# Attention scores as float32 matmuls of 64 rows in place of split operands of 128 rows

## The chip, the core and the metric

The kernel runs on one core of one Trainium2 chip. The metric is the device time of one execution in microseconds (us); the text gives the median of several runs. TensorE (PE in the rows; PEld is its weight load) multiplies matrices, VectorE (DVE), ScalarE (ACT) and GpSimd (POOL) work element by element, and the queue of SyncE (SP) issues nearly all transfers.

## The reference

Attention with a learned position bias feeds two gated feed-forward layers. Only the first part is touched by the change:

```python
B, H, S, D = q.shape                      # 2, 8, 576, 64
scores = np.matmul(q, k.transpose(0, 1, 3, 2)) / np.sqrt(D)
x = (log1p(abs(i - j)) / log1p(max(i, 1)))[..., None]
bias = np.maximum(x @ w1 + b1, 0.0) @ w2   # 32 hidden columns, one result for each head
scores = scores + bias.transpose(2, 0, 1)[None]
attn = softmax(scores)                     # over the last axis
out = np.matmul(attn, v)                   # then two gated layers, 512 -> 1536 -> 512
```

## The kernel before

Two heads form a pair, so a batch has four pairs (`hp` 0 to 3). The 576 rows of queries are cut into blocks, `it` 0 to 3 of 128 rows and `it` 4 of the last 64. A unit of work is a batch, a pair and a block: 40 units, the 20 of batch 0 first, with block 4 ahead of the others (`ITS`, L33; `UNITS`, L239 to L242). In a unit of 128 rows each of the two heads is a job `j`; in a unit of block 4 the two heads lie side by side in one tile of 128 rows.

The operands come from the array `qk`, which holds the 64 rows of a head's transposed queries (or keys) twice, one copy in partitions 0 to 63 and one in 64 to 127. `load_raw` (L122) issues one transfer for the queries and one for the keys of a pair. `split_set` (L140) then makes three float32r tiles: `qs`, whose upper half of partitions is the rounded query and whose lower half is the remainder, `kh`, the rounded key in both halves, and `kl`, the key's remainder in both halves. That is a copy each for `qs` and `kh` (L136 on ScalarE, L138 on GpSimd) and three subtractions (L150) for each pair and batch; `SPLIT0`, `SPLIT1` and `BOT0` say in which turn they are queued and on which engine, and `drain(poolq, ...)` issues them a few at a time. The raw tiles have one buffer of their own, and two more are borrowed from the tag `pt`.

`qk_mm` (L267) makes the scores. For 128 rows it issues four float32r matmuls for each job (L288): contraction 128, 128 columns of stationary `qs`, 288 moving columns of `kh`, then of `kl`, for each half of the keys. For block 4 it issues four plain float32 matmuls of contraction 64 from the raw tile (L276), the two heads going to the two halves of the output's partitions, that is, of the array's columns. A float32 matmul stands in the trace as two MATMUL records, a float32r one as one. The scores of one job take two of the four banks of the pool `ps2`.

A loop over turns `n` (L660) issues the parts of several units in an order written out by hand (`ORDERS`, L49): `M` adds scores and bias and takes the minimum on VectorE (L301), `X` is the exponential on ScalarE (L322), `N` the normalisation (L330, L332, and on GpSimd L334), `T` transposes unit n-3 on TensorE (L360), `E` takes the transposes out of PSUM, `P` and `V` are the product with the values (L380), `Q0` and `Q1` are the scores of unit n+1, `S0` and `S1` issue split work, `B` loads the bias of unit n+2, `L` loads operands, and `A`, `b`, `c` are steps of the position bias.

The bias is made once, for batch 0 and 1 together, in 36 groups of 16 rows: four hidden tiles a group, mostly on VectorE (L194), four matmuls (L208), a way out of PSUM (L212), a mirrored copy, mostly on GpSimd (L223), and a write to DRAM (L226), from which units read their rows (`bt`). Seven steps go ahead of the loop (`PRE`), the rest into turns 0 to 12. From turn 21 on, `C` converts the float64 weights of the layers to split float32 (L449 to L472). After the last unit come the 72 steps of the layers (L487, L512).

Every engine works its instructions off in the order in which they are issued.

Of the kernel before, what the change touches and what calls it, by code (L numbers as in the profile page):

```python
# [31 lines left out]
# order of the blocks of rows: the last 64 rows come first  # L32
ITS = (4, 0, 1, 2, 3)  # L33
# engines of the position bias: step -> hidden columns on ScalarE and on GpSimd (else VectorE);
# groups whose result leaves PSUM, or is mirrored, on VectorE (else ScalarE, GpSimd)
# [5 lines left out]
# turns of the attention loop that load and split operands: by pair of heads  # L41
RAW0 = {1: -3, 2: -2, 3: 1}
SPLIT0 = {0: -2, 1: -3, 2: -1, 3: 1}
BOT0 = ("gpsimd", "vector", "vector", "gpsimd")
LOAD1 = {10: 0, 20: 1, 24: 2, 29: 3}
SPLIT1 = {16: 0, 20: 1, 25: 2, 30: 3}
LOADV = {2: (0, 0), 3: (0, 1), 4: (0, 2), 5: (0, 3), 22: (1, 0), 25: (1, 1), 28: (1, 2), 32: (1, 3)}
# order in which a turn of the attention loop issues its parts
ORDERS = [  # L49
# [4 lines left out]
]  # L54
# float64's high word of the smallest normal float32, read as a float32
# [3 lines left out]
def rows_of(it):  # L59
    return 128 if it < 4 else 64  # L60


def bias_width(it):
    # distances j - i of a block of rows
    return S + rows_of(it) - 1
# [3 lines left out]
def fused_kernel(ctx: ExitStack, tc: tile.TileContext, qk, vp, tab, pcol, invp, prm, wts, rg, out):  # L69
# [18 lines left out]
    first = ExitStack()  # L88
    sb = first.enter_context(tc.tile_pool(name="sb", bufs=2, side="right"))
# [17 lines left out]
    # the tensor engine's clock rises with use: keep it busy until the first operands land  # L107
# [9 lines left out]
    # scores = [q_hi; q_lo] . [k_hi; k_hi] + [q_hi; q_lo] . [k_lo; k_lo]  # L117
    sets = {}
    raws = {}
    poolq = []  # L120

    def load_raw(b, hp, which, tag="raw", eng=nc.sync):  # L122
        if which == 0:
            raws[b, hp] = (wk if tag == "raw" else w2).tile([128, 4, S], F32, tag=tag, name=f"raw{b}{hp}", bufs=1 if tag == "raw" else 2)
        eng.dma_start(raws[b, hp][:, 2 * which : 2 * which + 2], qk[b, hp, which])
# [8 lines left out]
    def copy(o, i, eng):  # L134
        if eng == "act":
            nc.scalar.activation(o, i, AF.Copy)  # L136
        else:
            nc.gpsimd.tensor_scalar(o, i, 1.0, 1.0, op0=ALU.mult, op1=ALU.mult)  # L138

    def split_set(b, hp, copies, kl_eng, bot_eng):  # L140
        raw = raws[b, hp]
        qr, kr = raw[:, 0:2], raw[:, 2:4]
        pool = sb if b == 0 and hp >= 2 else wk
        qs = pool.tile([128, 2, S], F32R, tag="qs", name=f"qs{b}{hp}")
        kh = pool.tile([128, 2, S], F32R, tag="kh", name=f"kh{b}{hp}")
        kl = pool.tile([128, 2, S], F32R, tag="kl", name=f"kl{b}{hp}")
        sets[b, hp] = (qs, kh, kl)

        def low(o, i, h, eng):
            getattr(nc, eng).tensor_tensor(o, i, h.bitcast(F32), op=ALU.subtract)  # L150

        items = (
            lambda: copy(qs, qr, copies[0]),
            lambda: copy(kh, kr, copies[1]),
            lambda: low(qs[64:128], qr[64:128], qs[64:128], bot_eng),
            lambda: low(kl[:, 0], kr[:, 0], kh[:, 0], kl_eng[0]),
            lambda: low(kl[:, 1], kr[:, 1], kh[:, 1], kl_eng[1]),
        )
        poolq.extend(items)

# [5 lines left out]
    load_raw(0, 0, 0)  # L166
    load_raw(0, 0, 1)
# [5 lines left out]
    hts = {}  # L173

    # distances j - i from c0 on that a group's rows need on the longer side of the diagonal;
    # the bias depends on the distance's size only, so the other side is a mirror image
# [70 lines left out]
    def load_bias(n):  # L247
        b, hp, it = UNITS[n]
        bt = wk.tile([128, 2, S], F32, tag="bt", name=f"bt{n}", bufs=3)
        # row i starts i places to the left of the row before it  # L250
        w = bias_width(it)
        r = rows_of(it)
        flat = bias_d[it].rearrange("a w -> (a w)")
        for h in range(2 if it == 4 else 1):
            o = r - 1 + (2 * hp + h) * w
            rows = flat[o : o + r * (H * w - 1)].rearrange("(i k) -> i k", k=H * w - 1)
            if it == 4:
                nc.sync.dma_start(bt[h * 64 : h * 64 + 64, 0], rows[:, :S])
            else:
                nc.sync.dma_start(bt, rows[:, : 2 * w].rearrange("i (a k) -> i a k", a=2)[:, :, :S])  # L260
        st[n, "bt"] = bt

    # the last 64 rows of a pair's two heads go side by side: one tile of 128 rows
    def jobs(n):
        return 1 if UNITS[n][2] == 4 else 2

    def qk_mm(n, j):  # L267
        if j >= jobs(n):
            return
        b, hp, it = UNITS[n]  # L270
        sp = bank2(f"s{n}_{j}")
        if it == 4:
            raw = raws[b, hp]
            for hf in range(2):
                for h in range(2):
                    nc.tensor.matmul(  # L276
                        sp[h * 64 : h * 64 + 64, hf, :288],
                        raw[:64, h, 512:],
                        raw[:64, 2 + h, hf * 288 : hf * 288 + 288],
                        start=True,  # L280
                        stop=True,
                    )
        else:
            qs, kh, kl = sets[b, hp]
            lhs = qs[:, j, it * 128 : it * 128 + 128]
            for i, kk in enumerate((kh, kl)):
                for hf in range(2):
                    nc.tensor.matmul(  # L288
                        sp[:, hf, :288], lhs, kk[:, j, hf * 288 : hf * 288 + 288], start=(i == 0), stop=(i == 1)
                    )  # L290
        st[n, "s", j] = sp
# [151 lines left out]
    # float64 bits to float32: exponent and mantissa shifted into place, the low word's  # L443
    # rounded top bits added, values below the normal range set to zero
# [55 lines left out]
    def out_mm(s):  # L500
# [27 lines left out]
        # a bank's matmuls come before its readers, but at the end the readers run ahead  # L528
# [82 lines left out]
    # pieces go through a load and four steps, the steps of one turn each on another piece;  # L611
    # `limit`: pieces that have a free slot
# [18 lines left out]
    def raw0(n):  # L631
        for hp in range(1, 4):
            if RAW0[hp] == n:
                for i in range(2):
                    load_raw(0, hp, i, "raw" if hp == 3 else "pt")

    def split0(n):
        for hp in range(4):
            if SPLIT0[hp] == n:
                split_set(0, hp, ("act", "act" if hp == 0 else "pool"), ("gpsimd", "gpsimd"), BOT0[hp])  # L640

    raw0(-3)
    for i in range(PRE):
        bias_step()
        if i == 3:
            nc.vector.tensor_scalar(w1l[:, S:], w1l[:, S:], prms[:, 0:1], None, op0=ALU.mult)
            split0(-3)
        if i == 4:
            load_bias(0)
            qk_mm(0, 0)  # L650
            raw0(-2)
            split0(-2)
        if i == 6:
            load_bias(1)
            raw0(-1)
            split0(-1)
        if i > 3:
            drain(poolq, 3)

    for n in range(NU + TL + 1):  # L660
# [13 lines left out]
        def load_new():  # L674
            if n in LOAD1:
                for i in range(2):
                    load_raw(1, LOAD1[n], i)
            if n in LOADV:
                load_v(*LOADV[n])
            raw0(n)  # L680
            split0(n)
            if n in SPLIT1:
                split_set(1, SPLIT1[n], ("act", "pool"), ("vector", "gpsimd"), "gpsimd")

        def steps(k):
# [4 lines left out]
        dq = 3 if n < 25 else 2  # L690
# [17 lines left out]
            "Q0": lambda: n + 1 < NU and qk_mm(n + 1, 0),  # L708
            "Q1": lambda: n + 1 < NU and qk_mm(n + 1, 1),
            "S0": lambda: drain(poolq, dq - dq // 2),  # L710
            "S1": lambda: drain(poolq, dq // 2),
# [9 lines left out]
        if n == NB0:  # L721
            first.close()
            open_ring("mc", range(EARLY), "right")
# [110 lines left out]
```

## Time and profile before

| | |
|---|---|
| median of 3 runs | 691.87 us (688.51 to 692.51) |
| span of the profiled execution | 689.6 us |
| busy TensorE | 655.5 us, 95% |
| busy VectorE | 510.2 us, 74% |
| busy GpSimd | 354.4 us, 51% |
| busy ScalarE | 329.7 us, 48% |
| transfers | 87.06 MB, mean 126 GB/s |

For the profiled execution only its span is listed; the median of the runs is 2.3 us above it. A matmul's record includes its way through the array, and records overlap, so busy TensorE is not TensorE at its limit. Shares of the whole span are means over stages: the position bias and batch 0 (up to about 133 us), batch 1 (to about 209 us) and the layers (to the end).

### The profile page before, as it was taken

Reading aid. Unit: us, or ns where it says so; the run is one execution under the profiler, and the core shown is the slowest. Engines: PE = TensorE matmul, PEld = TensorE weight load, DVE = VectorE, ACT = ScalarE, POOL = GpSimd, SP = SyncE. Lnnn points to the kernel's source line nnn. Section 1 sums busy time; section 2 is a strip of 40 time slices with the busy share of each in tenths; the row PEclk is TensorE's granted clock in tenths of the full one; section 3 lists DMA queues with packets and bytes.
Section 4 is the critical chain, followed back from the end, with each engine's and each line's share of the span. In section 5 each row is a group of like instructions: output and inputs, shape, how many; then the busy total and the mean of one; then the engine's idle time right before and its main releaser. Section 6 shows DMA issues by size and latency. Waiting matters only on the chain.

```text
span 689.6 us, 11697 instructions
## 1 busy us (share of the span) xinstructions
PE 655.5 (95%) x4290; PEld 584.3 (85%) x4290; DVE 510.2 (74%) x941; ACT 329.7 (48%) x685; POOL 354.4 (51%) x336
## 2 busy tenths in 40 slices
PE   8779999988799799999999999989999999999997
PEld 4215567876678799989999999989999999999997
DVE  7899997578898986997677687989988778420121
ACT  5536678978786443444333345475443433211111
POOL 4557655889967453444434356665644444211111
PEclk9799999999999999999999999999999999999999
DMA  6659877689752332243223222232222221000111
GB/s 231 208 168 308 283 253 259 207 287 322 226 188 87 128 121 94 93 124 121 69 85 121 94 62 66 87 88 67 92 88 68 90 93 31 1 1 1 47 46 47
DMA packets 31641, 87.06 MB, mean 126 GB/s; under 512 B 3552, under 2 KB 5216, under 8 KB 31584
## 3 DMA queue, kind: packets, MB, share of 16 engines
q1 hardware_dynamic: 30720, 85.14, 37.9%
q10 hardware_dynamic: 864, 1.18, 0.5%
q8 instruction: 34, 0.56, 0.3%
q14 instruction: 23, 0.19, 0.1%
HBM read 73.05 MB, written 13.25 MB: 125 GB/s over the span
## 4 chain that ended last, share of the span: by engine, by line
PE 66%; DVE 17%; issue 5%; DMA 5%; ACT 3%; POOL 3%; SPq 0%; POOLq 0%; DVEq 0%; ACTq 0%
PE gv L487 35%; PE pv L380 4%; DVE ht L194 3%; PE tp L360 3%; PE s L288 3%; PE bps L208 3%; DVE ab L467 2%; DVE t L301 1%; DVE ff L460 1%; DMA bt<-bias_d 1%; DMA bias_d<-be 1%; DVE wv L472 1%; DVE tt L449 1%; DVE wl L472 1%; DVE rb L462 1%
## 5 line engine op out<-in xcount | busy, mean ns | idle before, releaser
L497 POOL TENSOR_TENSOR gl<-g,gh 128x384 fp32r<-128x384 f32 x72 | 89.2, 1239 | 180.7 <-ACT gh L495 180.7
L493 DVE TENSOR_TENSOR g<-gv,sg 128x384 f32<-128x384 f32 x72 | 40.0, 556 | 133.7 <-PE gv L487 122.6
L463 POOL TENSOR_TENSOR ff<-ff,rb 128x512 int32<-128x512 int32 x72 | 95.1, 1321 | 80.7 <-DVE rb L462 76.5
L495 ACT ACTIVATE gh<-g 128x384 fp32r<-128x384 f32 x72 | 37.9, 526 | 127.3 <-DVE g L493 126.6
L487 PE MATMUL gv<-xh,wl 128*128 128x384 f32 x240 | 80.8, 337 | 1.2 <-DVE wl L472 1.2
L487 PE MATMUL gv<-xh,wh 128*128 128x384 f32 x240 | 81.2, 338 | 0.0
L487 PE MATMUL gv<-xl,wh 128*128 128x384 f32 x240 | 80.7, 336 | 0.0
L334 POOL TENSOR_SCALAR p<-p,rs 128x576 f32<-128x576 f32 x72 | 65.1, 916 | 16.7 <-DVE rs L332 12.4
L194 DVE TENSOR_SCALAR ht<-w1l,bpc 128x448 f32<-128x448 f32 (+17 forms) x131 | 73.1, 624 | 0.3
L467 DVE SCALAR_TENSOR_TENSOR ab<-ab,ff 128x512 f32<-128x512 f32 x72 | 69.1, 959 | 0.0
L491 ACT ACTIVATE sg<-gv 128x384 f32<-128x384 f32 x72 | 35.0, 486 | 70.0 <-PE gv L487 69.5
L487 PE MATMUL gv<-nh,wh 128*128 128x384 f32 x192 | 64.8, 337 | 0.0
L468 ACT ACTIVATE wh<-ab 128x512 fp32r<-128x512 f32 x54 | 34.2, 633 | 63.9 <-DVE ab L467 63.6
L208 PE MATMUL bps<-ht,prms 128*32 128x264 f32 (+17 forms) x352 | 54.7, 530 | 10.5 <-DVE ht L194 8.6
L487 PE MATMUL gv<-nl,wh 128*128 128x384 f32 x192 | 64.5, 336 | 0.0
L487 PE MATMUL gv<-nh,wl 128*128 128x384 f32 x192 | 64.5, 336 | 0.0
L322 ACT ACTIVATE p<-t,mn 128x576 f32<-128x576 f32 x72 | 55.4, 770 | 13.1 <-DVE mn L301 11.2
L472 DVE TENSOR_TENSOR wl<-ab,wh 128x512 fp32r<-128x512 f32 x54 | 58.2, 1079 | 0.0
L462 DVE TENSOR_SCALAR rb<-wr 128x512 int32<-128x512 uint32 x72 | 56.9, 791 | 0.0
L301 DVE CUSTOM_DVE_ANT_0 t<-s,bt 128x576 f32<-128x576 f32 x72 | 51.7, 750 | 6.0 <-DMA bt<-bias_d 3.0
L460 DVE SCALAR_TENSOR_TENSOR ff<-wr,tt 128x512 uint32<-128x512 uint32 x72 | 54.3, 754 | 0.0
L360 PEld LDWEIGHTS tp<-ident,p 128*128 128x128 f32 (+1 forms) x328 | 36.0, 142 | 18.7 <-issue 6.7
(418 smaller groups left out, 1642.3 us busy)
## 6 DMA issues: line engine op xcount, KB each, us to landing
wr<-wts SPq DMA_DIRECT2D x72, 512.0 KB, 3.6
bt<-bias_d SPq DMA_DIRECT2D x32, 576.0 KB, 5.0
bias_d<-be SPq DMA_DIRECT2D x36, 295.5 KB, 3.2
raw<-qk SPq DMA_DIRECT2D x16, 576.0 KB, 5.6
v<-vp SPq DMA_DIRECT2D x8, 480.0 KB, 6.0
bt<-bias_d SPq DMA_DIRECT2D x16, 144.0 KB, 4.0
out<-part SPq DMA_DIRECT2D x6, 192.0 KB, 1.9
out<-part ACTq DMA_DIRECT2D x6, 192.0 KB, 1.9
```

The source lines that it names most:

```text
L194: nc.vector.tensor_scalar(ht, src, bpc[:, t : t + 1], 0.0, op0=ALU.add, op1=ALU.max)
L208: nc.tensor.matmul(ps[cg * 32 : cg * 32 + 32, :cut], prms[:, 2:34], hs[cg][:, a : a + cut], start=True, stop=True)
L301: nc.vector.tensor_tensor_reduce(t, sp[:, :, :288], bt[:, j].rearrange("p (a c) -> p a c", a=2), -SCALE, 3.0e38, ALU.add, ALU.min, mn[:, j ...
L334: nc.gpsimd.tensor_scalar(p[:, j], p[:, j], rs[:, j : j + 1], 1.0, op0=ALU.mult, op1=ALU.mult)
L360: nc.tensor.transpose(tp[:k, x * 128 : x * 128 + 128], blocks[i + x], ident)
L460: nc.vector.scalar_tensor_tensor(ff, hw, 0xC0000000, tt, op0=ALU.bitwise_and, op1=ALU.bitwise_or)
L462: nc.vector.tensor_scalar(rb, lw, 2.0**-29, None, op0=ALU.mult)
L463: nc.gpsimd.tensor_tensor(ff.bitcast(I32), ff.bitcast(I32), rb, op=ALU.add)
L467: nc.vector.scalar_tensor_tensor(ab, ab, TINY_HI, ff.bitcast(F32), op0=ALU.is_ge, op1=ALU.mult)
L472: nc.vector.tensor_tensor(lo, ab, hi.bitcast(F32), op=ALU.subtract)
L487: nc.tensor.matmul(ps[:, :CH], wt[:, cs], xt[:, cc, :], start=(k == 0), stop=(k == 11))
L497: nc.gpsimd.tensor_tensor(gl, g32, gh.bitcast(F32), op=ALU.subtract)
```

## The change

The split is gone, with its queue, its tiles, the pool `sb` and the parts `S0` and `S1`. `load_raw` now puts the queries and keys of a pair's first head into partitions 0 to 63 and those of its second head into 64 to 127 of one tile, half as many bytes, still in two transfers a pair; there are six such buffers. The loads of pair 3 of batch 0 move from turn 1 to ahead of the loop, those of pair 1 of batch 1 from turn 20 to turn 18. All scores are plain float32 matmuls of contraction 64: the first head on rows 0 to 63 of the array, the second on rows 64 to 127. `Q0` and `Q1` become one part `Q` that stands where `Q0` stood, except that `M1` now follows `M0` in three of the four orders.

```diff
-RAW0 = {1: -3, 2: -2, 3: 1}
-SPLIT0 = {0: -2, 1: -3, 2: -1, 3: 1}
-BOT0 = ("gpsimd", "vector", "vector", "gpsimd")
-LOAD1 = {10: 0, 20: 1, 24: 2, 29: 3}
-SPLIT1 = {16: 0, 20: 1, 25: 2, 30: 3}
+RAW0 = {1: -3, 2: -2, 3: -1}
+LOAD1 = {10: 0, 18: 1, 24: 2, 29: 3}
...
-    "M0 T X0 M1 N E0 B E2 E1 A L Q0 S0 X1 Q1 S1 P0 P1 b c V C",
-    "C M0 T L M1 X0 E0 Q0 X1 E2 A E1 B Q1 N P0 S0 P1 b V c S1",
-    "M0 X0 M1 C T Q0 N E1 E2 A B L E0 X1 Q1 P0 b S0 S1 P1 V c",
-    "M0 T X0 E2 N A Q0 E0 M1 C Q1 X1 E1 B L P0 S0 b P1 V S1 c",
+    "M0 M1 T X0 N Q E0 B E2 E1 A L X1 P0 P1 b c V C",
+    "C M0 M1 T L X0 E0 Q X1 E2 A E1 B N P0 P1 b V c",
+    "M0 M1 X0 C T Q N E1 E2 A B L E0 X1 P0 b P1 V c",
+    "M0 T X0 E2 N A Q E0 M1 C X1 E1 B L P0 b P1 V c",
...
+    def load_raw(b, hp):
+        t = wk.tile([128, 2, S], F32, tag="raw", name=f"raw{b}{hp}", bufs=6)
+        raws[b, hp] = t
+        for h in range(2):
+            r = slice(h * 64, h * 64 + 64)
+            nc.sync.dma_start(t[r], qk[b, hp][:, r, h].rearrange("w p s -> p w s"))
...
+    def qk_mm(n):
         b, hp, it = UNITS[n]
-        sp = bank2(f"s{n}_{j}")
+        raw = raws[b, hp]
+        sps = [bank2(f"s{n}_{j}") for j in range(jobs(n))]
         if it == 4:
...
+            order = [(h, hf, sps[0][h * 64 : h * 64 + 64, hf, :288]) for h in range(2) for hf in range(2)]
         else:
...
+            order = [(h, hf, sps[h][:, hf, :288]) for hf in range(2) for h in range(2)]
+        for h, hf, dst in order:
+            r = slice(h * 64, h * 64 + 64)
+            nc.tensor.matmul(
+                dst,
+                raw[r, 0, it * 128 : it * 128 + rows_of(it)],
+                raw[r, 1, hf * 288 : hf * 288 + 288],
+                start=True,
+                stop=True,
+            )
```

## Rows read from the trace of the kernel before

**Rows 1.** Windows by stage: us, busy time (instructions) by engine, TensorE's clock, DMA share, GB/s.
```profile
12.10:63.80 51.70, 41.91 (x250) 15.00 (x245) 48.77 (x91) 25.48 (x48) 33.39 (x30) 0.87 0.64 206
103.00:133.00 30.00, 29.66 (x295) 23.45 (x293) 20.42 (x65) 25.82 (x64) 19.85 (x26) 1.00 0.67 219
133.00:209.00 76.00, 67.94 (x628) 53.59 (x626) 63.17 (x160) 61.42 (x158) 64.30 (x72) 1.00 0.76 254
140.00:200.00 60.00, 51.94 (x465) 39.79 (x465) 52.80 (x131) 46.28 (x118) 51.20 (x53) 1.00 0.83 271
209.00:689.60 480.60, 468.63 (x2689) 462.13 (x2686) 333.25 (x510) 182.61 (x338) 208.62 (x163) 1.00 0.24 76
```

**Rows 2.** Timeline of VectorE, 12 to 64 us: start, duration, what, count.
```profile
12.74 3.43 DVE L194 TENSOR_SCALAR ht<-w1l,bpc 128x576 f32<-128x576 f32 x3
18.88 3.71 DVE L194 TENSOR_SCALAR ht<-w1l,bpc 128x560 f32<-128x560 f32 x3
22.59 1.32 DVE L194 TENSOR_SCALAR ht<-w1l,bpc 128x544 f32<-128x544 f32 x3
...
35.53 4.38 DVE L194 TENSOR_SCALAR ht<-w1l,bpc 128x480 f32<-128x480 f32 x4
...
45.36 8.18 DVE L194 TENSOR_SCALAR ht<-w1l,bpc 128x432 f32<-128x432 f32 x12
```

**Rows 3.** Timeline of GpSimd over the same stretch.
```profile
14.35 3.08 POOL L150 TENSOR_TENSOR kl<-raw,kh 128x576 fp32r<-128x576 f32 x2
19.11 2.76 POOL L150 TENSOR_TENSOR qs<-raw,qs 64x1152 fp32r<-64x1152 f32 x1 [1.68 <-ACT qs L136]
...
36.56 3.08 POOL L150 TENSOR_TENSOR kl<-raw,kh 128x576 fp32r<-128x576 f32 x2
...
48.82 2.62 POOL L150 TENSOR_TENSOR qs<-raw,qs 64x1152 fp32r<-64x1152 f32 x1
```

**Rows 4.** The splits by source line: duration min/median/max in ns, first and last start.
```profile
L150 POOL TENSOR_TENSOR kl<-raw,kh x12: 1399/1464/1849, 14.3 to 185.5; 128x576 fp32r<-128x576 f32 x12
L150 POOL TENSOR_TENSOR qs<-raw,qs x6: 2622/2634/3054, 19.1 to 180.1; 64x1152 fp32r<-64x1152 f32 x6
L150 DVE TENSOR_TENSOR kl<-raw,kh x4: 740/752/1294, 125.8 to 177.9; 128x576 fp32r<-128x576 f32 x4
L150 DVE TENSOR_TENSOR qs<-raw,qs x2: 1355/1356/1356, 17.5 to 40.1; 64x1152 fp32r<-64x1152 f32 x2
L138 POOL TENSOR_SCALAR kh<-raw x7: 1142/1157/1587, 12.9 to 175.9; 128x1152 fp32r<-128x1152 f32 x7
L136 ACT ACTIVATE qs<-raw x8: 1152/1157/1164, 14.2 to 175.6; 128x1152 fp32r<-128x1152 f32 x8
```

**Rows 5.** The chain that ended last, 40 to 64 us: start, us, what.
```profile
40.90 6.61 DMA raw<-qk
...
59.59 1.50 POOL kl L150
...
62.79 5.12 DMA bias_d<-be
```

**Rows 6.** Timeline of TensorE, one full turn near 121 us; block 4 at 144 us.
```profile
120.55 1.20 PE L360 MATMUL tp<-ident,p 128*128 128x128 f32 x9
121.51 0.51 PE L288 MATMUL s<-kh,qs 128*128 128x288 f32 x2
...
122.75 1.31 PE L380 MATMUL pv<-pt,v 128*64 128x128 f32 x20
123.99 1.20 PE L360 MATMUL tp<-ident,p 128*128 128x128 f32 x9
...
144.54 1.19 PE L276 MATMUL s<-raw 64*64 64x288 f32 x8 [1.01 <-DVE mn L301]
145.66 1.31 PE L380 MATMUL pv<-pt,v 128*64 128x128 f32 x20
```

**Rows 7.** Transfers by line: size of one, median us from issue to landing.
```profile
raw<-qk SPq DMA_DIRECT2D x16, 576.0 KB, 5.6
```

More of the change, by code (lines that the diff above doesn't have):

```diff
@@ L87, in fused_kernel @@
     wk = attn.enter_context(tc.tile_pool(name="wk", bufs=2))
-    first = ExitStack()
-    sb = first.enter_context(tc.tile_pool(name="sb", bufs=2, side="right"))
     prod = ExitStack()
@@ L114, in fused_kernel @@
     xl = [xp.tile([128, NCC, CH], F32R, tag="xl", name=f"xl{c}") for c in range(NCH)]
-    sets = {}
     raws = {}
[L120 to L125, printed above, removed]
+    def load_raw(b, hp):
[4 more added lines that the diff above has]
+            nc.sync.dma_start(t[r], qk[b, hp][:, r, h].rearrange("w p s -> p w s"))
     vs = {}
@@ L132, in load_v @@
         nc.sync.dma_start(vs[b, hp], vp[b, hp])
[L134 to L159, printed above, removed]
     def drain(q, k=99):
@@ L164, in drain @@
             k -= 1
-    load_raw(0, 0, 0)
-    load_raw(0, 0, 1)
+    load_raw(0, 0)
     nc.sync.dma_start(w1l[:, S:], tab[:, S:])
@@ L265, in jobs @@
         return 1 if UNITS[n][2] == 4 else 2
-    def qk_mm(n, j):
-        if j >= jobs(n):
-            return
+    def qk_mm(n):
         b, hp, it = UNITS[n]
-        sp = bank2(f"s{n}_{j}")
+        raw = raws[b, hp]
+        sps = [bank2(f"s{n}_{j}") for j in range(jobs(n))]
         if it == 4:
[L273 to L282, printed above, removed]
-        else:
[L284 to L291, printed above, removed]
+            order = [(h, hf, sps[0][h * 64 : h * 64 + 64, hf, :288]) for h in range(2) for hf in range(2)]
+        else:
+            order = [(h, hf, sps[h][:, hf, :288]) for hf in range(2) for h in range(2)]
[8 more added lines that the diff above has]
+            )
+        for j, sp in enumerate(sps):
+            st[n, "s", j] = sp
     def reduce_min(n, j):
@@ L633, in raw0 @@
             if RAW0[hp] == n:
[L634 to L640, printed above, removed]
+                load_raw(0, hp)
     raw0(-3)
@@ L646, in fused_kernel @@
             nc.vector.tensor_scalar(w1l[:, S:], w1l[:, S:], prms[:, 0:1], None, op0=ALU.mult)
-            split0(-3)
         if i == 4:
             load_bias(0)
-            qk_mm(0, 0)
+            qk_mm(0)
             raw0(-2)
-            split0(-2)
         if i == 6:
@@ L655, in fused_kernel @@
             raw0(-1)
-            split0(-1)
-        if i > 3:
-            drain(poolq, 3)
     for n in range(NU + TL + 1):
@@ L675, in load_new @@
             if n in LOAD1:
-                for i in range(2):
-                    load_raw(1, LOAD1[n], i)
+                load_raw(1, LOAD1[n])
             if n in LOADV:
                 load_v(*LOADV[n])
[L680 to L683, printed above, removed]
         def steps(k):
@@ L689, in fused_kernel @@
         live = n < NU
-        dq = 3 if n < 25 else 2
         pq = 5 if n < 34 else 10 if 36 <= n < 41 else 4
@@ L707, in fused_kernel @@
             "L": load_new,
[L708 to L711, printed above, removed]
+            "Q": lambda: n + 1 < NU and qk_mm(n + 1),
             "P0": lambda: drain(peq, pq - pq // 2),
@@ L721, in fused_kernel @@
         if n == NB0:
-            first.close()
             open_ring("mc", range(EARLY), "right")
```

## The prediction

> **What bounds the kernel now.** The windows by stage come first [rows 1], because a share of the whole span mixes three stages. In the first one shown, 12.1 to 63.8 us, VectorE is busy 48.8 of 51.7 us and TensorE only 41.9, much of that in waiting records: VectorE sets the pace. From 103 to 133 us TensorE is busy 29.7 of 30.0 and VectorE 20.4: TensorE sets it. From 133 to 209 us nobody is full over the whole stage; from 140 to 200 us TensorE is busy 51.9 of 60, VectorE 52.8, GpSimd 51.2, and the transfers take 0.83 of their engines. From 209 us on, the layers run, TensorE 468.6 of 480.6, and nothing of the change lies there; that stage starts earlier or later as a block.
>
> Next the timelines of VectorE and GpSimd are laid beside each other [rows 2, 3]. Three hidden tiles of 544 columns take 1.32 us at 22.59, when GpSimd does nothing: 0.44 each, 0.81 ns a column. Three of 576 take 3.43 us at 12.74, beside a key split on GpSimd that runs from 14.35 for 3.08 us; three of 560 take 3.71 us at 18.88, beside a query split of 2.76 us. So a split on GpSimd costs VectorE time although it isn't VectorE's instruction. The chain of waits shows two more places [rows 5]: a load of raw operands that is waited for (6.61 us from 40.90; it could not start before the single raw buffer was free), and a key split on GpSimd at 59.59 that stands ahead of a bias write.
>
> **The change part by part.** *Splits removed.* On GpSimd twelve `kl`, six `qs` and seven `kh` go: 12 x 1.46 + 6 x 2.63 + 7 x 1.16 = 41.5 us; on ScalarE eight `qs` copies and one `kh`, about 9 x 1.16 = 10.4 us; on VectorE two `qs` of 1.36 and four `kl` of 0.75 or more [rows 4]. All of that is gain only where it is on the path.
>
> In 12 to 64 us VectorE is on it. Two `qs` are 2.7 us directly. The stretching: at 0.81 ns a column the four stretched groups should take 1.40, 1.36, 1.55 and 4.20 us; they take 3.43, 3.71, 4.38 and 8.18 [rows 2], together 11.2 us more. Beside the first, second and most of the third and fourth runs a split [rows 3], but other GpSimd work (normalisation, mirrors) has a share too, so I count 9.5 us. Together 12.2 us of VectorE time. Not all of it becomes time of the end: the next limits of the stage are the transfers (0.64 of 51.7 = 33 us) and the way of the bias through DRAM (5.12 us for a single write [rows 5], then its read). I take **10 us**, with 5 and 16 as ends: 5 if those latencies take over soon, 16 if the raw wait and the whole 11.2 come on top of the 2.7.
>
> In 133 to 209 us TensorE idles 8.1 of the 60 us from 140 to 200 [rows 1]; no more than that can be won, whatever gets lighter. Removed there are half of the GpSimd splits, some 20 us, VectorE's 4 x 0.75 = 3 us, and half the bytes of the raw loads: of sixteen transfers of 576 KB [rows 7] the six of pairs 1 to 3 of batch 1 fall here, 3.5 MB, half of which at 271 GB/s is 6.5 us of transfer time. Since three resources near their limit get lighter at once, I take half of the idle time, **4 us** (0 to 8).
>
> *Scores of 128 rows.* The trace shows no matmul on rows 64 to 127 alone. What it shows is two matmuls on two halves of the columns. Nine transposes of 128 columns start at 120.55 and end their pace at 121.51: 0.107 us for each record. The product with the values has twenty records of that width, 2.13 us one after the other; from its start to the next transposes it takes 123.99 - 122.75 = 1.24 us [rows 6]. So the halves run two at a time, with 0.17 us for changing the shape. The scores of block 4, eight records of 288 columns, would need 8 x 0.24 = 1.92 us in a row and take 145.66 - 144.54 = 1.12. Now the float32r scores of a turn take 122.75 - 121.51 = 1.24 us. If halves of the rows pair as halves of the columns do, the new scores take 1.12 and, as they now differ in shape from the transposes ahead of them, up to 0.17 more: 1.29, which is 0.05 more than now. Over the 8 turns from 103 to 133 us and the 16 wide units of batch 1 that is **+1 us** at most. I take this end, the paired one, because block 4 is the nearest row in width, type and contraction. The other end, one after the other, is a rival below.
>
> The Trainium skill says that a change of tiling mode drains TensorE ("TensorEngine Tiling (Array Packing)", Key Properties), which speaks against the change, since each wide unit gets one more. The trace agrees with a small price, the 0.17 above; with it the sum is as it stands, without it 1 us lower.
>
> *Scores of block 4.* Their order turns from half by half to head by head, so the first head's two matmuls stand ahead of the second's. Ends: still paired, 0; nothing paired, 1.92 - (1.12 - 0.17) = 1 us each. Four of the eight units lie in batch 1, where TensorE is closer to its limit: I take half, **+2 us** (0 to 4). In the first stage TensorE has room for the other four.
>
> *Loads and queue.* With six buffers no raw load waits for a free one; pair 3's load moves from turn 1 to ahead of the loop, which SP's queue passes without a wait, and the bias writes behind it no longer stand behind a waiting load. Its cost is nothing as long as the early transfers (0.64 busy) have room; that is inside the 5 to 16.
>
> *Q in one piece.* The second head's scores now wait for `M1` of the unit before, already at Q's place, and the bias products of part `A` queue behind them on TensorE. VectorE does `M0` and `M1` back to back at the start of its turn, some 1.4 us, while TensorE has the transposes and the product before it, 0.96 + 1.24 us [rows 6]. I count nothing; if VectorE is late in a turn, it costs up to the difference.
>
> **The sum** goes by the profiled span: 689.6 - 10 - 4 + 1 + 2 = 678.6 us. The median of the runs is 2.3 us above that span; so 691.9 - 11 = 681 us, rounded to **681**.
>
> **The rivals.** *Row halves do not pair.* Each wide unit then takes 1.92 + 2 x 0.17 = 2.26 us, 1.0 more than now. From 103 to 133 us TensorE is full, so 8 x 1.0 = 8 us. In batch 1 it is 16 x 1.0 + 4 x 1.0 = 20, less the 8 us idle, 12, and the gain of 4 is lost. In the first two stages TensorE has room: the 10 stay. 692 - 10 + 8 + 12 = **702 us**. It decides from about 0.5 us more a unit, where the 20 wide and late units cost what the first stage gives. For it: no row shows the second half of rows in use. Against it: the pairs of column halves, which stream two operands as these would. Chance 0.14. The skill's page named above states that tiles work independently and in parallel, rows as well as columns; no run so far shows it for rows.
>
> *The freed time is not collected.* VectorE is freed, but the bias' way through DRAM (5.12 us a write) and the transfers set the first turns, and batch 1 stays held by its bias loads at 0.83 busy: -5, -1, +1 and +2 make about **688 us**, within 1%. For it: the chain in that stage passes through transfers; against it: VectorE is busy 94% of the stage, and when it stretches, GpSimd is at work on a split. Chance 0.16.
>
> *My forecast's mechanism*, 0.70, by itself 671 to 685: 16 and 8 at one end, 7 and 1 with the costs at the other.
>
> **Numbers.** About 1%, 7 us, is what a measurement can tell from no change. Faster by more (under 685): 0.70, slower by more (over 699): 0.14, between: 0.16. The range takes in the second case and most of the way to the first rival, 670 to 698; some 0.05 lies below, 0.14 above.
>
> **What would show it.** In the trace after: no L150, L136 or L138; hidden tiles at 0.4 to 0.5 us where they took 1.1; TensorE full about 10 us before 103 us, and the layers begun 10 to 14 us before 209 us; no wait for a raw load; the scores of a turn at 1.1 to 1.3 us with starts in pairs. A turn near 115 us that takes 4.4 us in place of 3.44 would show the first rival. GpSimd still stretching VectorE in the first 50 us, by mirrors and normalisation alone, would show that I put the stretch on the wrong instructions.

## The result, and the profile after

The changed kernel takes 673.7 us in the median of 4 runs (670.93 to 675.25), the kernel before 691.15 us in its runs beside them (688.51 to 692.51). The ratio is 0.9744, with a 95% interval of 0.9705 to 0.9784: 17.5 us faster. The forecast was 681 us with a range of 670 to 698, faster by 11 us.

The profiled execution after has a span of 668.7 us. Against 689.6 that would be 20.9 us, 3 more than the medians differ, so the two traces are compared stage by stage. The profiled execution of one experiment (GpSimd's part on ScalarE) was disturbed, and neither its time nor a line of it is used. Here are the windows of the kernel after (us, busy time and instructions of TensorE, its weight load, VectorE, ScalarE and GpSimd, then TensorE's clock, the share of the transfers, GB/s), cut where the same work begins and ends as in [rows 1]:

```profile
12.10:51.00 38.90, 33.51 (x247) 13.24 (x242) 31.47 (x93) 20.65 (x44) 13.37 (x18) 0.96 0.79 250
88.00:119.40 31.40, 31.40 (x302) 21.67 (x301) 19.92 (x65) 25.77 (x64) 15.72 (x27) 1.00 0.72 215
119.40:190.00 70.60, 70.28 (x625) 48.48 (x624) 54.28 (x157) 57.66 (x155) 42.89 (x60) 1.00 0.78 241
190.00:668.70 478.70, 468.52 (x2689) 462.30 (x2687) 333.67 (x510) 182.30 (x338) 208.81 (x163) 1.00 0.25 76
```

The boundaries are those of the reductions on VectorE and of the first matmul of the layers: the unit that opens the TensorE-bound stage (turn 12) is reduced at 102.91 us before and at 87.85 after; batch 1 begins at 133.2 before and 119.4 after; the layers begin at 209.0 and 190.0.

| stretch | before | after | change |
|---|---|---|---|
| to turn 12 | 102.91 | 87.85 | -15.1 |
| turns 12 to 19 | 30.3 | 31.5 | +1.2 |
| batch 1, to the layers | 75.8 | 70.6 | -5.2 |
| the layers | 480.6 | 478.7 | -1.9 |

The timeline of VectorE (start, duration, what, count) shows most of the first line. These are the groups of hidden tiles that answer to [rows 2]:

```profile
12.14 1.38 DVE L161 TENSOR_SCALAR ht<-w1l,bpc 128x576 f32<-128x576 f32 x3
...
13.80 1.35 DVE L161 TENSOR_SCALAR ht<-w1l,bpc 128x560 f32<-128x560 f32 x3
...
15.38 1.33 DVE L161 TENSOR_SCALAR ht<-w1l,bpc 128x544 f32<-128x544 f32 x3
...
28.03 2.00 DVE L161 TENSOR_SCALAR ht<-w1l,bpc 128x480 f32<-128x480 f32 x4
...
35.38 4.77 DVE L161 TENSOR_SCALAR ht<-w1l,bpc 128x432 f32<-128x432 f32 x12
```

The group of 544 columns, which had GpSimd idle beside it before, is unchanged (1.32 and 1.33 us). The other four took 3.43, 3.71, 4.38 and 8.18 us, together 19.70, and now take 9.50. The same instruction over the whole span, before and then after (ns: shortest, median, longest):

```profile
L194 DVE TENSOR_SCALAR ht<-w1l,bpc x131: 357/486/2865, 5.6 to 108.7; 128x512 f32<-128x512 f32 x8, 128x480 f32<-128x480 f32 x8, 128x464 f32<-128x464 f32 x8, 128x448 f32<-128x448 f32 x8
```

```profile
L161 DVE TENSOR_SCALAR ht<-w1l,bpc x131: 361/468/968, 5.0 to 94.2; 128x512 f32<-128x512 f32 x8, 128x480 f32<-128x480 f32 x8, 128x464 f32<-128x464 f32 x8, 128x448 f32<-128x448 f32 x8
```

The shortest and the median barely move; the longest falls from 2.87 us, about the length of a query split on GpSimd [rows 4], to 0.97. So a stretched VectorE instruction seems to hold its wait for GpSimd inside its busy time; the trace shows no idle time for it.

TensorE's timeline has one full turn of the second line of the table, and a unit of block 4, as in [rows 6]:

```profile
102.80 1.20 PE L322 MATMUL tp<-ident,p 128*128 128x128 f32 x9
103.93 1.24 PE L245 MATMUL s<-raw 64*128 64x288 f32 x8
105.10 1.31 PE L342 MATMUL pv<-pt,v 128*64 128x128 f32 x20
106.34 1.20 PE L322 MATMUL tp<-ident,p 128*128 128x128 f32 x9
...
118.11 1.19 PE L245 MATMUL s<-raw 64*64 64x288 f32 x8
119.24 0.98 PE L342 MATMUL pv<-pt,v 128*64 128x128 f32 x14
```

The new scores take 105.10 - 103.93 = 1.17 us and the whole turn 3.54 in place of 3.44: eight records of 288 columns in the time of four. The block of 64 rows takes 1.13 us as before (1.12), although its order is now head by head.

The first stage also differs in TensorE's clock: 0.96 of full speed in the first window above, 0.87 in that of [rows 1]. Over 12.1 to 103 us it is 0.98 against 0.91, with TensorE busy for 84.9 against 79.5 us. The prediction has no term for it.

### The profile page after: what moved, and what is told of

It reads as the page before. It is cut to its first block, busy times and chain, and to the rows that moved or that the text cites. A ratio compares the mean times of both kernels' runs of the same rounds, so it can differ in the third digit from the quotient of the medians.

```text
span 668.7 us, 11610 instructions
## 1 busy us (share of the span) xinstructions
PE 650.6 (97%) x4290; PEld 573.0 (86%) x4290; DVE 483.0 (72%) x935; ACT 320.0 (48%) x676; POOL 307.8 (46%) x311
## 4 chain that ended last, share of the span: by engine, by line
PE 78%; DVE 12%; issue 3%; ACT 2%; DMA 2%; POOL 1%; SPq 0%; POOLq 0%; ACTq 0%; DVEq 0%
PE gv L449 35%; PE s L245 7%; PE pv L342 7%; PE tp L322 6%; PE bps L175 4%; DMA bias_d<-be 2%; DVE ab L429 2%; DVE ff L422 1%; DVE wv L434 1%; DVE ht L161 1%; DVE tt L411 1%; DVE g L455 1%; DVE rb L424 1%; DVE wl L434 1%; POOL gl L459 1%
## 5 line engine op out<-in xcount | busy, mean ns | idle before, releaser
L425 POOL TENSOR_TENSOR ff<-ff,rb 128x512 int32<-128x512 int32 x72 | 95.1, 1321 | 79.4 <-DVE rb L424 75.8
L296 POOL TENSOR_SCALAR p<-p,rs 128x576 f32<-128x576 f32 x72 | 60.8, 855 | 19.0 <-DVE rs L294 15.9
L263 DVE CUSTOM_DVE_ANT_0 t<-s,bt 128x576 f32<-128x576 f32 x72 | 51.8, 752 | 17.5 <-PE s L245 10.7
L161 DVE TENSOR_SCALAR ht<-w1l,bpc 128x448 f32<-128x448 f32 (+17 forms) x131 | 60.1, 523 | 2.0 <-PE bps L175 1.9
L245 PE MATMUL s<-raw 64*128 64x288 f32 (+1 forms) x320 | 56.9, 428 | 1.5 <-DVE mn L263 1.5
L424 DVE TENSOR_SCALAR rb<-wr 128x512 int32<-128x512 uint32 x72 | 54.9, 763 | 0.0
L342 PEld LDWEIGHTS pv<-pt,v 128*64 128x64 f32 (+1 forms) x640 | 34.2, 136 | 18.8 <-ACT pt L623 6.3
```

The lines of the kernel that those rows point to most:

```text
L161: nc.vector.tensor_scalar(ht, src, bpc[:, t : t + 1], 0.0, op0=ALU.add, op1=ALU.max)
L245: nc.tensor.matmul(dst, raw[r, 0, it * 128 : it * 128 + rows_of(it)], raw[r, 1, hf * 288 : hf * 288 + 288], start=True, stop=True,)
L296: nc.gpsimd.tensor_scalar(p[:, j], p[:, j], rs[:, j : j + 1], 1.0, op0=ALU.mult, op1=ALU.mult)
L342: nc.tensor.matmul(box["ps"][j * 64 : j * 64 + 64, :n], v[:k, 2 * j if it == 4 else j, c, :], pt[:k, c, j * 64 : j * 64 + 64] if it == 4 e ...
L424: nc.vector.tensor_scalar(rb, lw, 2.0**-29, None, op0=ALU.mult)
L425: nc.gpsimd.tensor_tensor(ff.bitcast(I32), ff.bitcast(I32), rb, op=ALU.add)
```

## The experiments

All ratios are to the kernel before, with 95% intervals; the changed kernel's is 0.9744. In us, a ratio's distance from that is taken of 691.

**The whole split as dead work.** `split_set`, its queue and its turns stand as before, and nothing reads the tiles. In this run and the others with dead work the tiles of the split stand in fewer buffers than the real ones did, and the raw tiles have five in place of six.

```diff
+            split0(-3)
...
+            lambda: copy(qs, raw, copies[0]),
+            lambda: copy(kh, raw, copies[1]),
+            lambda: low(qs[64:128], raw[64:128], qs[64:128], bot_eng),
+            lambda: low(kl[:, 0], raw[:, 0], kh[:, 0], kl_eng[0]),
+            lambda: low(kl[:, 1], raw[:, 1], kh[:, 1], kl_eng[1]),
```

> The changed kernel with the whole split of the kernel before put back as dead work, on the same engines and in the same turns; no matmul reads it. Theory (the gain is the split's work, above all GpSimd's, which stretches VectorE): nearly all of the 17.5 us comes back, 686 to 691 us, the hidden tiles of the bias take about 0.62 us in the mean again (0.52 without the split) and the first block of 128 rows is reduced near 57 us again (44 without it). Rival (the gain is the scores themselves and the loads, which this run keeps as changed): 674 to 678 us.

Measured: 690.81 us, ratio 1.0005 (0.9979 to 1.0031). Everything is given back: with the split in place the new scores and the halved loads gain nothing, so there is no gain without the split's removal. Turn 12 is reached 16.5 us later than in the changed kernel, the hidden tiles take 0.607 us in the mean, and the first block of 128 rows is reduced at 60.2 us.

**GpSimd's part alone, VectorE's and ScalarE's part alone.** Each piece reads the raw tile alone, so that it needs no other engine's result:

```diff
+        def low(o, i, eng):
+            if eng == "gpsimd":
+                nc.gpsimd.tensor_tensor(o, i, i, op=ALU.subtract)
```

> Only GpSimd's part of the split is put back as dead work (7 copies, 18 subtractions, which read the raw tile alone and so wait for no other engine). Theory: GpSimd's work is most of it, 683 to 688 us, VectorE's hidden tiles at 0.60 us or more in the mean. Rival (VectorE's and ScalarE's own split instructions and the waits between engines were the cost): under 678 us and hidden tiles still at 0.52 to 0.54.

> Only VectorE's part (2 of 64x1152, 4 of 128x576, some 5.7 us) and ScalarE's (9 copies, 10.4 us) are put back as dead work. Theory: +2 to +5 us, that is 676 to 679 us, since 2.7 us of VectorE's work lie in the stage that it bounds. Rival of the run before: +9 us or more, 683 us and above.

Measured: 680.16 us (0.9848, 0.9817 to 0.9879) and 673.17 us (0.9756, 0.9725 to 0.9787): 7 us and 1 us, the second not to be told from nothing and less than the 2 to 5 us that I expected. The first, too, is less than I expected, and more than its rival allows. The rows by line, with busy us and mean ns, say where it sits: the hidden tiles with GpSimd's part, with the other part, and in the changed kernel.

```profile
L193 DVE TENSOR_SCALAR ht<-w1l,bpc 128x448 f32<-128x448 f32 (+17 forms) x131 | 68.7, 589 | 2.2 <-PE bps L207 2.1
```

```profile
L193 DVE TENSOR_SCALAR ht<-w1l,bpc 128x448 f32<-128x448 f32 (+17 forms) x131 | 59.2, 517 | 2.6 <-PE bps L207 2.4
```

```profile
L161 DVE TENSOR_SCALAR ht<-w1l,bpc 128x448 f32<-128x448 f32 (+17 forms) x131 | 60.1, 523 | 2.0 <-PE bps L175 1.9
```

In the kernel before this line has 73.1 us. GpSimd's pieces lengthen VectorE's own work by 8.6 us, and turn 12 comes 6.8 us later; 5.9 us of further instructions on VectorE and 10.4 on ScalarE do next to nothing. A subtraction that reads one tile twice is shorter on GpSimd than the real one, so this run puts back 37.4 of the 42.9 us of GpSimd's split work. The longest hidden tile is shorter with it, 2.35 us in place of 2.87, as are the query pieces, 2.25 us in place of 2.63 in the median.

**GpSimd's part on ScalarE.** A control: the same pieces, as copies on ScalarE.

> The same pieces as in the run with GpSimd's part, put on ScalarE as copies (about 22 us of ScalarE's time in place of 42 us of GpSimd's); nothing reads them. Theory (VectorE is stretched by what runs on GpSimd at the same time, not by reads of the same tile or by load on any engine): hidden tiles stay at 0.52 to 0.54 us and the time rises by 0 to 4 us, to 674 to 678 us. Rival (any further work beside VectorE, or ScalarE's queue that also takes the bias out of PSUM, costs as much): 680 us or more.

Measured: 673.21 us, a ratio of 0.9744 (0.9719 to 0.9769), the changed kernel's own. What the hidden tiles took in it was not seen. The pieces cost 7 us on GpSimd and nothing on ScalarE.

**All pieces, each from the raw tile alone.**

> All pieces of the split as dead work on all three engines, but each reads the raw tile alone, so that no piece waits for another engine's. GpSimd's pieces alone cost 6.5 us, VectorE's and ScalarE's alone nothing, the coupled split 17. Theory (the other 10 us are the waits between engines: GpSimd and VectorE standing in their queues for a copy that ScalarE has not reached): 680 to 683 us. Rival (the pieces load three engines at once and add up beyond their single costs even without waits): 686 to 691 us.

Measured: 683.39 us (0.9905, 0.9881 to 0.993): 11 us, where the single parts add up to 8 and the coupled split costs 18. So 3 us come with all the pieces together. In the same run VectorE's own four `kl` pieces take 1.51 us in the mean, where they take 0.80 without GpSimd's. That leaves 7 us between this run and the coupled split, and the waits between engines are only one of three differences.

The waits are not all gone in this run. ScalarE's copy and the lower half of `qs` write one tile, and GpSimd stands before that half as long as in the kernel before. What goes is the wait before pair 0's `kl`, for which the kernel before needs ScalarE's `kh`. First three rows of the kernel before, then the two pieces in this run:

```profile
19.11 2.76 POOL L150 TENSOR_TENSOR qs<-raw,qs 64x1152 fp32r<-64x1152 f32 x1 [1.68 <-ACT qs L136]
26.44 2.77 POOL L150 TENSOR_TENSOR kl<-raw,kh 128x576 fp32r<-128x576 f32 x2 [4.58 <-issue]
...
25.15 1.16 ACT L136 ACTIVATE kh<-raw 128x1152 fp32r<-128x1152 f32 x1
```

```profile
18.20 2.42 POOL L138 TENSOR_TENSOR qs<-raw 64x1152 fp32r<-64x1152 f32 x1 [1.93 <-issue]
20.70 2.34 POOL L138 TENSOR_TENSOR kl<-raw 128x576 fp32r<-128x576 f32 x2
```

The trace names nobody for the 4.58 us, but they end just after that copy, at 26.31. The coupled dead split has the same wait of 4.58 us. Its second unit is reduced at 34.18 us and that of this run at 31.19, after a first one at 24.11 and 24.17: 3 of the 7 us arise there.

The second difference is that GpSimd's pieces are shorter here, 36.8 against 42.2 us in all. The third is TensorE's clock. From the third unit's reduction to the fifth's the coupled split takes 16.2 us and this run 12.8. From 40 to 62 us the granted clock was 0.69 in the one and 1.00 in the other, so that TensorE stood at the lower of its two levels (1.2 and 2.4 GHz) for some 13.6 us. From 50 to 55 us it had been busy for only 1.8 us, 3.17 us of that stretch idle until VectorE had reduced earlier scores, and from 55 to 60 us the clock was 0.50. The windows, coupled and then each piece from the raw tile:

```profile
40.00:62.00 22.00, 17.20 (x78) 6.59 (x80) 18.72 (x45) 7.93 (x16) 11.47 (x12) 0.69 0.54 176
```

```profile
40.00:62.00 22.00, 19.22 (x140) 8.16 (x141) 21.07 (x58) 11.80 (x24) 14.54 (x17) 1.00 0.75 244
```

How much of the 7 us each of the three carries was not separated.

**Both heads on the same rows.** The second head's scores are computed from the first head's operands, so that both use rows 0 to 63.

```diff
-            r = slice(h * 64, h * 64 + 64)
+            r = slice(0, 64)
```

> Both heads' scores read rows 0 to 63 of the array, so the second head's scores are those of the first, computed twice; the number and shape of matmuls stays, but for 128 rows no two can run side by side on halves of the rows. Theory (halves of the rows pair): the scores of a full turn take 2.1 to 2.3 us in place of 1.17, a turn near 105 us 4.5 us in place of 3.55, and the time rises by 8 us for the TensorE-bound turns of batch 0 and 16 us for batch 1, to 692 to 700 us. Rival (they don't run side by side in the changed kernel either, the time is won elsewhere): no change, 672 to 676 us.

Measured: 694.74 us (1.0061, 1.003 to 1.0093), 22 us slower than the changed kernel and slower than the kernel before. The timeline of TensorE shows a turn of 114.59 - 110.08 = 4.51 us, with 2.13 for the scores:

```profile
110.08 1.20 PE L322 MATMUL tp<-ident,p 128*128 128x128 f32 x9
111.22 2.21 PE L245 MATMUL s<-raw 64*128 64x288 f32 x8
113.35 1.31 PE L342 MATMUL pv<-pt,v 128*64 128x128 f32 x20
114.59 0.66 PE L322 MATMUL tp<-ident,p 128*128 128x128 f32 x4
```

Same matmuls, same shape, 2.13 against 1.17 us: the two halves of the rows do run side by side, and without that the change would have been a loss. By the traces 4.4 us are lost before turn 12, 6.8 in turns 12 to 19 and 12.4 in batch 1.

**The loads.** First, each raw load twice, the second into a tile that nothing reads; then the same with pair 3 of batch 0 in turn 1; then only pair 3 in turn 1, single.

```diff
+        more = wk.tile([128, 2, S], F32, tag="more", name=f"more{b}{hp}", bufs=2)
+        for h in range(2):
+            r = slice(h * 64, h * 64 + 64)
+            nc.sync.dma_start(more[r], qk[b, hp][:, r, 1 - h].rearrange("w p s -> p w s"))
```

> Each raw load is followed by two more of 288 KB into a tile that nothing reads, so that the bytes are those of the kernel before. Theory (the transfers have room; fewer bytes were a small part of the gain): 674 to 677 us. Rival (half the bytes of the loads were a main part, 4.6 MB at some 270 GB/s being 17 us of transfer time): 680 us or more, with waits for the bias loads in batch 1.

> As the run with doubled loads, but pair 3 of batch 0, with its second load, in turn 1 as in the kernel before. Theory (once the split is gone the transfers are the next limit of the first stage, and the bytes matter wherever they stand): 682 to 687 us. Rival (the 13 us of the doubled loads were only pair 3's bytes ahead of the loop, in front of the first bias writes): 675 to 679 us.

> Pair 3 of batch 0 is loaded in turn 1 again in place of ahead of the loop, with a free buffer. Theory: the place of the load costs little once no buffer is waited for, 674 to 677 us. Rival (the 6.61 us that the chain of the kernel before shows in that load were won by its place): 678 to 681 us.

Measured: 686.96 us (0.9924, 0.99 to 0.9948), 684.81 us (0.9922, 0.9886 to 0.9958) and 676.31 us (0.9772, 0.9728 to 0.9815): 12, 12 and 2 us, the last not to be told from nothing. My theory of room fell: the bytes of the kernel before cost 12 us, wherever they stand. They come in 32 transfers of 288 KB here, in 16 of 576 KB there; bytes and number of transfers were not separated. By line, with those who waited for it (us, times), the bias writes of the changed kernel and then with doubled loads; the last line of each is the time to landing, shortest, median and longest.

```profile
L193 SPq DMA_DIRECT2D bias_d<-be x36: 319/320/622, 9.1 to 96.9; - x36
...
  ACT be L179: 3.7, 3
...
DMA to landing us min/median/max: 2.1/3.8/6.6
```

```profile
L197 SPq DMA_DIRECT2D bias_d<-be x36: 319/320/592, 8.9 to 106.1; - x36
...
  ACT be L183: 16.5, 5
  POOL be L194: 5.4, 1
...
DMA to landing us min/median/max: 2.1/4.9/8.1
```

The bias rows have three buffers. When a write takes 4.9 us in place of 3.8, ScalarE waits 16.5 us in place of 3.7 for one of them to come free, and VectorE is busy only 22.3 of the 37.9 us from 12.1 to 50 us (30.6 in the changed kernel). Turn 12 comes 9.2 us later. Batch 1 then takes 77.2 us in place of 70.6, with the waits for the bias loads that the rival had named: here those of 119 to 190 us in the changed kernel, then of 128 to 206 us with doubled loads.

```profile
DVE t L263 <- DMA bt<-bias_d: 1.3, 1, 1.3
```

```profile
DVE t L267 <- DMA bt<-bias_d: 12.2, 3, 4.9
```

Yet with the split in place the halved loads gained nothing (the first run). Two limits lie close to each other, the split and the transfers; the change lifted both. Lifted alone, the transfers won nothing, and the split about 5 us.

**Two attempts at more.** Scores of batch 1 behind half of the product with the values; the early queries of batch 0 loaded later; both.

```diff
-    "M0 M1 X0 C T Q N E1 E2 A B L E0 X1 P0 b P1 V c",
+    "M0 M1 X0 C T N E1 E2 A B L E0 P0 Q X1 b P1 V c",
...
+                nc.sync.dma_start(t[r, 1], qk[b, hp, 1, r, h])
+                nc.sync.dma_start(t[r, 0, 512:], qk[b, hp, 0, r, h, 512:])
```

> In batch 1 the scores of the next unit stand behind half of the product with the values, so that the second head's scores wait less for VectorE's second reduction. Some ten turns show 1.5 to 1.9 us in place of 1.17 for the scores, some 5 us in all. Theory (that time is a real loss on TensorE): 2 to 4 us faster, 670 to 672 us. Rival (VectorE then gets its scores later and waits as long): 673 to 677 us.

> In batch 0 the queries of rows 0 to 511, which nothing reads before turn 3, are loaded in turns 0 to 3; ahead of the loop come the keys and the last 64 queries alone, 1 MB less of early transfers. Theory (transfers set the first turns now): 2 to 4 us faster, 669 to 672 us. Rival (the rest collides later, or its own six transfers a pair cost SP's queue as much): 673 to 676 us.

> The run before with the late scores of batch 1 added, which by themselves gave 672.3 us. Theory (both gains are real and lie in different stages): 668 to 671 us. Rival: not below the run before by more than 1 us.

Measured: 672.26 us (0.9706, 0.9661 to 0.9752), 674.02 us (0.9769, 0.9742 to 0.9795) and 672.36 us (0.9743, 0.9718 to 0.9767). None can be told from the changed kernel. In the first, batch 1 takes 70.5 us, against 70.6 without the edit; in the second, the first turns are 0.7 us earlier (the first wide unit at 43.7 in place of 44.4 us) and by turn 12 0.8 us later. A megabyte less ahead of the loop is not worth its six transfers a pair; the 12 us above are not a line on which each megabyte has its price. No version was found that beats the changed kernel.

## Why the prediction was right, and where it was off

*The mechanism was right.* GpSimd's splits stretched VectorE in a stage that VectorE bounds. The four groups lost 10.2 us where I counted 9.5, and the runs with dead work on GpSimd and on ScalarE show that it is GpSimd, not load as such. The Trainium skill states a reason ("SBUF — State Buffer", the section "SBUF: two separate sides"): VectorE and GpSimd share a port pair, which a GpSimd instruction, or a VectorE instruction of certain modes, holds as a whole while the other waits, and ScalarE has ports of its own. The runs agree: 7 us on GpSimd, none on ScalarE, and single stretched tiles about as long as a GpSimd instruction. But GpSimd's pieces by themselves account for 7 of the 17.5 us, and for the rest of what the coupled split costs the share of each cause is open.

*The first stage was mis-sized:* 10 us taken, 15.1 measured to turn 12, near the end of 16 that the term had. I took 10 of the 12.2 us counted, because the bias' way through DRAM would take over. That limit was there, as the doubled loads show, but the change moved it as well, and I had not put the two together: I priced the halved bytes of the loads in batch 1 alone, and with the split gone the doubled loads delay turn 12 by 9.2 us. The term for pair 3's place held: loaded in turn 1 again it costs 2 us, not to be told from nothing. VectorE's own two `qs`, counted at 2.7 us, were worth less: with all of VectorE's and ScalarE's pieces put back, turn 12 comes 1.4 us later. Nor did I count what the coupled split costs beyond the same pieces from the raw tile alone, 7.4 us to turn 12: a wait of 4.58 us on GpSimd, longer pieces and TensorE's lower clock, unseparated.

*The scores of a turn* were forecast 0.05 us dearer and are 0.10 dearer a turn (3.54 against 3.44); turns 12 to 19 grew by 1.2 us in all, where the forecast's +1 covered batch 1 too. The step from column halves to row halves held. The first rival's price, 21 us above the forecast, came out as 22 us above the changed kernel in the run on the same rows: its mechanism and, in the main, its size were right, and only its condition did not hold. It had nothing for the first stage, where 4.4 us were lost, and 8 for turns 12 to 19, where it was 6.8.

*The scores of block 4* were forecast at +2 and cost nothing: eight records in 1.13 us, where one after the other they would take 1.92. So they are paired, although the kernel issues the second head's matmuls after both of the first. It follows that TensorE did not start these matmuls strictly in the kernel's order, as the text ahead of the prediction has it for every engine; that order mattered less than I had assumed.

*Batch 1* went from 75.8 to 70.6 us, -5.2, where -4 and the +2 stood, and most of the +1. TensorE is now busy 70.3 of these 70.6 us: the stage has become what I called its limit. Its idle time fell from 8.1 to 0.3 us, of which I had taken only 4. Its busy time grew by some 2.5 us, about what the forecast had there; as block 4 costs nothing, that agreement is luck.

*Two sums* of the prediction are off by 1 or 2 us: the second rival's, 691.9 - 5 - 1 + 1 + 2, is 689 and not 688, and the slow end of my own mechanism, 691.9 - 7 - 1 + 1 + 2, is 687 and not 685. Neither changes what the result says.

*The layers* were to shift as a block, and did. Their 480.6 and 478.7 us differ, though nothing of them was edited (see below).

## What to carry to other kernels

Read a timeline of two engines side by side before an instruction's mean is believed: the same VectorE instruction took 0.46 or 1.14 us, and the trace showed no wait, only what GpSimd did at that time. When work is removed from a stage, price the second limit with the change applied, too; here the work and the transfers were both lifted. Putting back the transfers alone cost 12 of the 17.5 us, putting back the work alone all of it. When dead work is put back, look in its trace for the waits that it was meant to leave out: one of them was still there. Plain float32 matmuls of contraction 64 on each half of the rows cost nearly the same as split operands of contraction 128 (a turn of 3.54 against 3.44 us), and the elementwise work of splitting was the real price.

## What the runs showed that I had not expected

The costs were far from additive: GpSimd's part 7 us, the other part 1, both from the raw tile alone 11, the coupled split 18; the loads nothing beside the split and 12 us without it.

The layers did not take the same time in all traces, though nothing of them was edited. By their first matmul and the span it is 480.6 us before, 478.7 in the changed kernel, 478.7 to 478.8 with the coupled split, with GpSimd's part and with both heads on the same rows, and 480.3 with doubled loads and with the pieces from the raw tile alone. That accounts for 1.9 of the 3.4 us by which the two profiled executions differ more than the medians. What decides it was not tried.
